# Gated linear attention and a two-layer MLP on one core: two tokens to a partition, one logarithm for both, quarter-tile scores, single PSUM banks, five early loads on ScalarE's DMA ring

## The chip, the cores and the metric

The kernel runs on one core of a Trainium2 chip. The metric is the device time of one execution in microseconds, and less is better. The profile is one execution taken by the hardware profiler; its span is measured from the first to the last instruction. The engines are named as in the profile: PE (TensorE), PEld (its weight loads), DVE (VectorE), ACT (ScalarE), POOL (GpSimd) and SP (SyncE).

## The reference

There are 4 batches, 8 heads, 768 tokens and 48 channels per head. Attention is a recurrence with a forget gate per channel; its output, with the heads side by side, goes through a layer of 384 to 2048, a smooth gate, and a layer of 2048 to 384.

```python
f = 1.0 / (1.0 + np.exp(-f_logit))
for t in range(S):
    state = f[:, :, t, :, None] * state + einsum('bhd,bhe->bhde', k[:, :, t], v[:, :, t])
    y[:, :, t] = einsum('bhd,bhde->bhe', q[:, :, t], state)
x = y.transpose(0, 2, 1, 3).reshape(B * S, H * D)
h = x @ w_in
g = 0.5 * (h + np.sqrt(h * h + 4.0))
return g @ w_out
```

## The kernel before

The 3072 tokens are cut into 24 blocks of 128 tokens, one token to a partition, and two blocks make a pair p (12 pairs, three to a batch). `add_load` reads f, q, k and v of a pair, each with two DMAs of 128 partitions x 8 heads x 48 floats, so each piece in memory is 192 bytes (L363).

**Logs and decays.** `add_logs` takes the exponential of -f (L425) and ln(1 + that) (L430), both over 768 columns, on ACT, and splits the result into a high (L433) and a low (L436) 16-bit part. `add_decays` sums the logarithms along the block with a centred triangular matrix on PE (L467, L468) into `hps`, adds small matmuls with `hvec` for the sums of each half block (L473, L474), takes exponentials of the sums with both signs on ACT (`ea` and `eap`, L481), and multiplies q by one and k by the other (`qk`, L487). v is cast to 16 bits (L494). `add_gammas` turns the half-block sums into the decay of the state from block to block (`nls` L499, `gi` L538, `gam` L547).

**Attention.** `add_attention` transposes q and k of a block, on PE (L593, copy L597) for pairs 0 to 4 and by DMA (L581) for pairs 5 to 11. Scores of two heads at a time go to two PSUM tiles (`sc`, L618: matmuls of 48 rows, in the upper and in the lower half of the array), are masked on DVE (`pm`, L625), and are multiplied by v; a term with the state is added (`y`, L639 and L641). `add_state` forms the next state (`u` L703 and L706, `sn` L710). y is cast (L648 or L650) and transposed, on PE (L683, L686) or by DMA (L673), into `xT`.

**MLP.** `add_mlp1` runs eight half steps per pair, each of six matmuls of 256 columns (L740). ACT squares the result (`hsq`, L746) and takes the square root of two half steps at a time (`r`, L755), and DVE joins them to the gated value (`g`, L763). `add_mlp2` multiplies by `w_out` in four quarters of four matmuls of 384 columns for each block (`o`, L780), copies the sum to `o_sb` on ACT or DVE (L789, L791), and stores it (L795).

**Order.** No scheduler of the language is at work. A planner of the kernel, `Plan`, is given each piece of work with its engine, a duration, what it depends on and a due time from the tables `BASE` and `SHIFT`; it plays the engines forward, and then the pieces are emitted in the order found. The engine of a piece that has a choice is in the table `ENG`. Loads, DMA transposes and stores share SP's queue, in order; weights are loaded and cast by POOL's queue (L388). PSUM is divided into pools, five banks for `hps`, two for attention, one for `o`:

```python
NH, NA, NO = 5, 2, 1
```

f has three load buffers, and q, k and v have four each; `o_sb` has two buffers of one block. ACT changes its function table between exponential/logarithm and square root where the planner's order asks for it (L841, L843).

Of the kernel before, what the change touches and what calls it, by code (L numbers as in the profile page):

```python
# [15 lines left out]
GROUPS = [[0], [1], [2], [3], [4], [5, 6], [7, 8], [9, 10], [11]]  # L16

XBAR = [5, 6, 7, 8, 9, 10, 11]

BASE = {  # L20
    "A": [-91.5, -48.2, -86.7, 59.5, 5.1, 3.6, 35.4, 93.4, 55.3, 161.2, 112.5, 128.2],
    "B": [-33.0, -23.9, 18.0, -28.5, -32.3, 71.1, -18.2, 43.6, 49.9, 25.6, 129.6, 106.7],
    "M": [63.0, -3.2, -1.9, 48.3, 21.6, 51.8, 114.9, 66.8, 229.7, 86.1, 210.4, 238.2],
    "O": [63.2, 45.4, 128.9, 46.1, 124.2, 143.7, 179.0, 123.5, 212.6, 237.4, 202.6, 191.4],
}
PART = {n: k for k, v in {
    "A": "W hi lo qk v16 nls gam", "B": "T SC KV Y Yc YT xq xy", "M": "M1 M R G", "O": "M2 ev out"}.items()
    for n in v.split()}

SHIFT = {  # L30
    "ld": 25.6, "win": 4.5, "wout": 7.0, "W": -4.7, "hi": 73.7, "lo": -32.1, "qk": -11.9, "v16": -32.1,
    "nls": -54.3, "gam": -112.9, "T": -87.4, "xq": -171.2, "SC": 9.3, "Y": -140.2, "Yc": 36.7, "YT": 70.6,
    "xy": 89.2, "KV": 58.5, "M1": 3.8, "M": 94.0, "R": -53.7, "G": -57.6, "M2": 33.2, "ev": -104.7,
    "out": 212.9,
}

NEAR = {'PE': 0.02, 'ACT': 0.1, 'DVE': 0.05, 'POOL': 0.3, 'SP': 0.2}

ENG = {
    "hi": "DDDDPDPPPPPP",  # L40
    "lo": "PPPDPPPDPPPD",
    "qk": "PPPPDPDDPDPP",
    "v16": "PDPPDPPPPPPP",
    "T": "DDADDDDDDDAAADDADDADDDDD",
    "Yc": "AADDADDDDDDDDDADDDDDDDDD",
    "ev": "DDDDDADDDDDDDADADAADAAAA",
}
FULL = {"D": "DVE", "A": "ACT", "P": "POOL"}

FINE = [0]  # L50

START = {"POOL": 3.8, "DVE": 3.6, "PE": 3.4, "ACT": 0.7, "SP": 0.7}

AFTER = {'in': 0, 'out': 2}


NH, NA, NO = 5, 2, 1

WDMA, VDMA = True, False

ORDER = "P0 P1 i03 f2 i47 o07 qkv2"


class Op:
    __slots__ = ("eng", "dur", "deps", "emit", "due", "allocs", "uses", "end", "kind", "dma", "ins", "flow", "issued")

    def __init__(self, eng, dur, emit, deps=(), due=0.0, allocs=(), uses=(), kind=None, dma=None, ins=()):
        self.eng, self.dur, self.emit, self.due, self.kind, self.dma = eng, dur, emit, due, kind, dma
        self.deps = [d for d in deps if d is not None]
        self.allocs, self.uses = list(allocs), list(uses)  # L70
        for b in self.uses:
            b.users.append(self)
        self.end = None
        self.ins = list(ins)
        self.flow = None


class Ring:
    def __init__(self, n, ordered):
        self.n, self.bufs, self.ordered, self.made = n, [], ordered, 0  # L80


class Buf:
    def __init__(self, ring):
        self.ring, self.users = ring, []
        self.seq = ring.made
        ring.made += 1


class Plan:  # L90

    HOP = 0.22
    TABLE = 1.3

    def __init__(self):
        self.queues = {}
        self.order = []

    def add(self, queue, eng, dur, emit, p=None, at=None, due=0.0, **kw):
        if isinstance(dur, dict):
            eng = FULL[ENG[queue][p if at is None else at]]
            dur = dur[eng]
        due += SHIFT.get(queue, 0.0) + (0.0 if p is None else BASE[PART[queue]][p])
        op = Op(eng, dur, emit, due=due, **kw)
        self.queues.setdefault((eng, queue), []).append(op)
        return op

    def ready(self, op):  # L110
        t = 0.0
        for d in op.deps:
            if d.end is None:
                return None
            t = max(t, d.end + (0.0 if d.eng == op.eng and d.dma is None else self.HOP))
        for b in op.allocs:
            r = b.ring
            k = len(r.bufs) - r.n
            if r.ordered and b.seq != len(r.bufs):
                return None  # L120

            k += sum(1 for x in op.allocs[:op.allocs.index(b)] if x.ring is r)
            if k >= 0:
                for u in r.bufs[k].users:
                    if u.end is None:
                        return None
                    t = max(t, u.end + (0.0 if u.eng == op.eng and u.dma is None else self.HOP))
        return t

    def flows(self):  # L130


        todo = {"SP": [], "POOL": []}
        for op in self.order:
            if not isinstance(op, str) and op.dma is not None:
                todo[op.eng].append([op.issued, op.dma[0], op])
        t = 0.0
        while todo["SP"] or todo["POOL"]:
            live = {e: q[0] for e, q in todo.items() if q and q[0][0] <= t + 1e-9}
            later = [q[0][0] for e, q in todo.items() if q and e not in live]  # L140
            if not live:
                t = min(later)
                continue
            rate = {"SP": 0.35, "POOL": 0.65} if len(live) == 2 else {e: 1.0 for e in live}
            step = min([x[1] / rate[e] for e, x in live.items()] + [a - t for a in later])
            t += step
            for e, x in live.items():
                x[1] -= step * rate[e]
                if x[1] <= 1e-9:
                    x[2].flow = t + x[2].dma[1] - x[2].issued  # L150
                    todo[e].pop(0)

    def run(self, passes=3):
        for n in range(passes):
            for ops in self.queues.values():
                for op in ops:
                    op.end = None
                    for b in op.uses + op.allocs:
                        b.ring.bufs = []
            self.order = []  # L160
            self.once()
            if n + 1 < passes:
                self.flows()

    def once(self):
        heads = {k: 0 for k in self.queues}
        free = dict(START)
        dma_free = 0.0
        table = None
        left = sum(len(v) for v in self.queues.values())  # L170
        by_eng = {}
        for k in self.queues:
            by_eng.setdefault(k[0], []).append(k)
        stretch = None
        loose = False
        while left:
            best = None
            for eng, ks in by_eng.items():
                now = free.get(eng, 0.0)
                cands = []  # L180
                for k in ks:
                    if heads[k] < len(self.queues[k]):
                        op = self.queues[k][heads[k]]
                        t = self.ready(op)
                        if t is not None:
                            cands.append((max(now, t), op, k))
                if not cands:
                    continue
                if eng == "PE" and stretch is not None and not loose:

                    if any(heads[k] < len(self.queues[k]) and self.queues[k][heads[k]].kind == ("W", stretch)
                           for k in ks):
                        cands = [c for c in cands if c[2][1] != "M1" or not c[1].allocs]
                        if not cands:
                            continue
                if eng == "ACT" and stretch is None and not loose:

                    opened = []
                    for c in cands:
                        if c[1].kind is not None and c[1].kind[0] == "W":  # L200
                            ins = [d for o in self.queues[c[2]][heads[c[2]]:heads[c[2]] + 16]
                                   if o.kind == c[1].kind for d in o.ins]
                            if any(d.end is None for d in ins):
                                continue
                            c = (max([c[0]] + [d.end - 1.0 for d in ins]),) + c[1:]
                        opened.append(c)
                    cands = opened
                    if not cands:
                        continue
                if eng == "ACT":  # L210

                    if stretch is not None and not loose:
                        mine = [c for c in cands if c[1].kind == ("W", stretch)]
# [662 lines left out]
```

## Time and profile before

The time before is 229.51 us, the median of two runs (228.28 to 230.74).

| | from the profile |
|---|---|
| span | 228.4 us, 4796 instructions |
| busiest engines | PE 186.2, ACT 168.7, DVE 157.0, POOL 75.1 us |
| mean granted PE clock | 0.963 |
| DMA | 129303 packets, 32.10 MB, 121088 of the packets under 512 B |
| ACT table loads | 16, of 1283 ns each |
| first matmul of the first layer | at 24.16 us |

A busy time is the union of an engine's instructions. A matmul's end is modelled, so a busy PE is not a PE at its peak. Where a row gives a mean for matmuls, it is longer than the distance from one start to the next, because they overlap. An idle engine costs something only where it is the one the others wait for.

### The profile page before, as it was taken

The page shows a single profiled execution, that of the slowest core. Times are in us where ns is not written, and L with a number is a line of the kernel's source. Part 1 is how long each engine was busy: PE and PEld are TensorE (multiplying, and loading weights), DVE is VectorE, ACT ScalarE, POOL GpSimd, SP SyncE. Part 2 cuts the span into 40 slices and gives each one's busy share as a digit, 9 for nine tenths or more (in the row PEclk, how much of TensorE's full clock was granted, in tenths as well). Part 3 has the DMA queues.
Part 4 walks back from the last instruction along what each step waited for, and adds up shares of the span by engine and source line. Part 5 has one row for each costly group of instructions (what it writes and reads, how often), then busy time and mean ns, then how long its engine had stood idle before and what let it go on. Part 6 is the DMA issues. An engine that isn't in the chain of part 4 may idle for free.

```text
span 228.4 us, 4796 instructions
## 1 busy us (share of the span) xinstructions
PE 186.2 (82%) x1870; PEld 133.3 (58%) x1870; DVE 157.0 (69%) x295; ACT 168.7 (74%) x258; POOL 75.1 (33%) x74
## 2 busy tenths in 40 slices
PE   0456858589998499599449999699999999999983
PEld 0243636357666257477326766576777777777641
DVE  6154286699895469598155998489989899855420
ACT  5333395999999918399705998599799999999820
POOL 5799426560640449610000692012504200000000
PEclk9999997999999589999967999999999999999999
DMA  7999999999998998999980569411193532010101
GB/s 140 207 194 188 178 208 181 204 155 202 189 222 170 230 209 175 247 171 220 220 207 1 124 139 207 102 52 55 52 195 76 119 47 57 17 54 34 70 34 69
DMA packets 129303, 32.10 MB, mean 141 GB/s; under 512 B 121088, under 2 KB 129280, under 8 KB 129280
## 3 DMA queue, kind: packets, MB, share of 16 engines
q1 hardware_dynamic: 123904, 28.65, 63.6%
q0 software_dynamic: 5376, 3.15, 9.5%
q8 instruction: 14, 0.23, 0.4%
q14 instruction: 9, 0.07, 0.1%
HBM read 25.17 MB, written 4.72 MB: 131 GB/s over the span
## 4 chain that ended last, share of the span: by engine, by line
PE 57%; ACT 16%; DVE 7%; DMA 6%; POOL 5%; SPq 4%; issue 3%; POOLq 0%; ACTq 0%; DVEq 0%
PE o L780 23%; PE hps L740 22%; ACT hsq L746 5%; DMA out_dram<-o_sb 4%; ACT r L755 4%; SPq L363 4%; PE sc L618 2%; DMA xT<-y 2%; DVE pm L625 2%; POOL w_in L388 2%; POOL qk L487 2%; PE hps L468 2%; ACT L843 2%; PE hps L467 1%; PE y L641 1%
## 5 line engine op out<-in xcount | busy, mean ns | idle before, releaser
L780 PE MATMUL o<-w_out,g 128*128 128x384 f16 x384 | 76.0, 335 | 14.7 <-DVE o_sb L791 13.5
L740 PE MATMUL hps<-xT,w_in 128*128 128x256 f16 x576 | 75.0, 282 | 3.7 <-DMA xT<-y 2.3
L763 DVE SCALAR_TENSOR_TENSOR g<-hps,r 128x512 f16<-128x512 f32 x96 | 61.6, 683 | 12.7 <-ACT r L755 12.3
L746 ACT ACTIVATE hsq<-hps 128x512 f16<-128x512 f32 x96 | 53.8, 591 | 22.0 <-PE hps L740 21.0
L740 PEld LDWEIGHTS <-w_in 128*128 128x128 f16 x576 | 56.7, 101 | 15.8 <-issue 5.0
L780 PEld LDWEIGHTS <-g 128*128 128x128 f16 x384 | 36.3, 100 | 34.8 <-issue 17.5
L755 ACT ACTIVATE r<-hsq 128x1024 f16<-128x1024 f16 x48 | 50.7, 1057 | 1.3
L625 DVE TENSOR_TENSOR pm<-sc,mask 128x512 f16<-128x512 f32 x48 | 31.1, 683 | 9.0 <-PE sc L618 9.0
L494 POOL CAST v<-ld_v 128x768 f16<-128x768 f32 (+1 forms) x11 | 8.5, 771 | 57.6 <-PE y L641 36.8
L487 POOL TENSOR_TENSOR qk<-ld_q,ea 128x768 f16<-128x768 f32 (+1 forms) x9 | 14.7, 1631 | 34.9 <-ACT ea L481 33.5
L481 ACT ACTIVATE ea<-hps 128x384 f32<-128x384 f32 x24 | 10.6, 491 | 12.1 <-PE hps L474 12.1
L791 DVE COPY o_sb<-o 128x384 f32<-128x384 f32 x15 | 8.3, 554 | 15.7 <-DMA out_dram<-o_sb 14.9
L436 POOL TENSOR_TENSOR llo<-ls,lhi 128x768 f16<-128x768 f32 (+1 forms) x10 | 15.3, 1534 | 9.8 <-DVE gam L547 6.2
L487 POOL TENSOR_TENSOR qk<-ld_k,eap 128x768 f16<-128x768 f32 (+1 forms) x9 | 15.4, 1712 | 0.0
L425 ACT ACTIVATE ld_f<-ld_f 128x768 f32<-128x768 f32 (+1 forms) x13 | 10.5, 804 | 4.6 <-DMA ld_f<-in_f_logit_dram 4.6
L467 PE MATMUL hps<-lhi,wcent 128*128 128x384 f16 x24 | 8.9, 370 | 5.8 <-DVE lhi L433 5.8
L618 PE MATMUL sc<-qkT 48*128 48x128 f16 x192 | 11.0, 228 | 2.4 <-DVE pm L625 1.1
L710 DVE TENSOR_TENSOR sn<-u,gam 128x384 f16<-128x384 f32 x20 | 11.0, 549 | 2.4 <-PE u L706 2.3
L641 PE MATMUL y<-v,pm 128*128 128x48 f16 x192 | 11.8, 187 | 0.4 <-DVE pm L625 0.4
L597 DVE COPY qkT<-tr 128x1024 f16<-128x1024 f16 x9 | 6.0, 685 | 8.7 <-PE tr L593 8.7
L641 PEld LDWEIGHTS <-pm 128*128 128x128 f16 x192 | 10.2, 99 | 3.0 <-issue 1.3
L618 PEld LDWEIGHTS <-qkT 48*128 48x128 f16 x192 | 6.2, 98 | 9.5 <-issue 8.0
(55 smaller groups left out, 217.5 us busy)
## 6 DMA issues: line engine op xcount, KB each, us to landing
ld_f<-in_f_logit_dram SPq DMA_DIRECT2D x24, 192.0 KB, 4.0
ld_q<-in_q_dram SPq DMA_DIRECT2D x24, 192.0 KB, 3.8
ld_k<-in_k_dram SPq DMA_DIRECT2D x24, 192.0 KB, 3.8
ld_v<-in_v_dram SPq DMA_DIRECT2D x24, 192.0 KB, 3.9
out_dram<-o_sb SPq DMA_DIRECT2D x24, 192.0 KB, 2.2
w_in<-in_moe_w_in_dram POOLq DMA_DIRECT2D x8, 192.0 KB, 7.7
w_out<-in_moe_w_out_dram POOLq DMA_DIRECT2D x8, 192.0 KB, 6.8
qkT<-qk SPq DMA_TRANSPOSE x14, 3.3
```

Source lines behind the costliest of these rows:

```text
L436: eng_of[lg[p, x].eng].tensor_tensor(out=llo[p % NL][:, x:y, :, 0:D], in0=T["ls", p][:, x:y], in1=lhi[p % NL][:, x:y, :, 0:D], op=ALU.subt ...
L467: nc.tensor.matmul(out=ca, lhsT=wcent, rhs=lhi[p % NL][:, r, :, 0:D], start=True, stop=False)
L487: eng_of[mu[p, x, i].eng].tensor_tensor(out=qk[p % NB][:, x:y, i, :, 0:D], in0=T[name, p][:, x:y], in1=T[e, p][:, x:y], op=ALU.mult)
L618: nc.tensor.matmul(out=T["sc", r, s][:, j, :], lhsT=qkT[o:o + D, NP + j, :], rhs=qkT[o:o + D, j, :], start=True, stop=True)
L625: nc.vector.tensor_tensor(out=T["pm", r][:, s], in0=T["sc", r, s], in1=mask16.unsqueeze(1).broadcast_to([128, NP, C]), op=ALU.mult)
L641: nc.tensor.matmul(out=y[:, j, s], lhsT=T["pm", r][:, s, j, :], rhs=T["v16", p][:, i, 2 * j + s, :], start=(c == 0), stop=(c == 0 or s == 1))
L710: nc.vector.tensor_tensor(out=T["sn", r + 1], in0=T["u", r], in1=gam[b % 2][:, c].unsqueeze(3).broadcast_to([128, NP, 2, D]), op=ALU.mult)
L740: nc.tensor.matmul(out=hb[:, a, :], lhsT=w_in16[j2][:, j, a * 128:(a + 1) * 128], rhs=T["xT", p][:, j, :], start=(j == 0), stop=(j == NJ - 1))
L746: nc.scalar.activation(out=T["hsq", p, j4][:, a], in_=T["h", p, j2], func=AF.Square, scale=1.0)
L755: nc.scalar.activation(out=T["r16", p, j4], in_=T["hsq", p, j4], func=AF.Sqrt, scale=0.25, bias=1.0)
L763: nc.vector.scalar_tensor_tensor(out=T["g", p][:, jn:jn + 2, :].rearrange("p a t -> p (a t)"), in0=T["h", p, 2 * j4 + a], scalar=0.5, in1= ...
L780: nc.tensor.matmul(out=T["o", p, i], lhsT=T["g", p][:, jn, i * C:(i + 1) * C], rhs=w_out16[jn // 2][:, jn % 2, :], start=(jn == 0), stop=( ...
```

## The change

Nothing in the result changes, but the work is cut in another way, and the planner is gone: the order of all pieces, the engine of each, and the PSUM banks of each that needs some are written out as a list of words (`ORDER`), which is played through once. `lq0.0:A` means the load of q, pair 0, first half, issued by ACT; `cu0.0:T@01` means the cumulative sums on PE into banks 0 and 1.

**Two tokens to a partition.** A pair of 256 tokens is loaded with one DMA for each of f, q, k and v. Partition p holds tokens 2p and 2p+1, which lie side by side in memory, so a piece is 384 bytes. Partitions 0 to 63 hold the first 128 tokens, and 64 to 127 the others. The loads have three buffers each.

**One logarithm for both.** With e = exp(-f), u = 1 + e is formed for both tokens (`ut`), multiplied together (`tt`), and one logarithm is taken of the product, so cumulative sums and their exponentials are of two-token steps. What the single tokens lack is multiplied in directly: q of the even token by the odd one's u (`qu`), k by u or by the product (`ku`), before the old multiplications by the exponentials (`qm`, `km`).

**Quarter-tile scores.** A score matmul has 48 rows and 64 columns of weights, for a head of two and for one of the two blocks, so four lie side by side in the array. Transposes, v products and state updates use the upper or lower 64 rows.

**Single banks.** Every PSUM tile is one of eight banks, named in the order. **Five early loads** (`lq0.0`, `lq0.1`, `lv0.0`, `lv0.1`, `lq1.0`) are issued by ACT ahead of its first exponential. DMA transposes serve pairs 4 to 11 instead of 5 to 11. A pair's output is stored from a buffer of both blocks, of which there are two, in two DMAs of 64 partitions.

```diff
-GROUPS = [[0], [1], [2], [3], [4], [5, 6], [7, 8], [9, 10], [11]]
-XBAR = [5, 6, 7, 8, 9, 10, 11]
-NH, NA, NO = 5, 2, 1
+XBAR = [4, 5, 6, 7, 8, 9, 10, 11]
+DEPTH = {'f': 3, 'q': 3, 'k': 3, 'v': 3, 'UT': 2, 's': 2, 'ep': 2, 'ea': 2, 'v16': 4, ... 'xT': 5, 'hsq': 2, 'r16': 2, 'g': 4, 'os': 2}
+ORDER = """
+lf0.0:S lf0.1:S lf1.0:S lk0.1:S lk0.0:S TABLE:e lq0.0:A lq0.1:A lv0.0:A lv0.1:A lq1.0:A ex0.0:A ut0.0:P ex0.1:A tt0.0:D
...
+"""
...
+                    eng(e).dma_start(out=T[s, p][:, hs].rearrange("p h i d -> p h (i d)"),
+                                     in_=src[s][bb][hs, t0:t0 + 256, :].rearrange("h (p i) d -> p h (i d)", i=2))
...
+                eng(e).tensor_scalar(out=T["UT", p][:, 0::2, hs], in0=T["f", p][:, hs].rearrange("p h i d -> p i h d"),
+                                     scalar1=1.0, scalar2=None, op0=ALU.add)
...
+                mul(e, u[:, 1, hs], u[:, 0, hs], u[:, 2, hs])
...
+                nc.scalar.activation(out=T["s", p][:, hs], in_=T["UT", p][:, 1, hs], func=AF.Ln)
...
+                t = T["q", p][:, hs, 0, :]
+                mul(e, t, t, T["UT", p][:, 2, hs])
...
+                t = T["k", p][:, hs].rearrange("p h i d -> p i h d")
+                mul(e, t, t, T["UT", p][:, 0:2, hs])
...
+                for j in range(4):
+                    for h in range(2):
+                        for cc in range(2):
+                            r = slice(64 * h, 64 * h + D)
+                            t = T["qkT", p, cc]
+                            nc.tensor.matmul(out=T["sc", p, i, h][64 * cc:64 * cc + 64, j, :],
+                                             lhsT=t[r, 1, j, i, :], rhs=t[r, 0, j], start=True, stop=True)
```

## The prediction

> **What bounds the kernel now.** I read the busy table first, then the 40 slices, then a table of stretches, the waits and the chain.
>
> ```profile
> PE 186.2 (82%) x1870; PEld 133.3 (58%) x1870; DVE 157.0 (69%) x295; ACT 168.7 (74%) x258; POOL 75.1 (33%) x74
> ...
> PE   0456858589998499599449999699999999999983
> ...
> PEclk9999997999999589999967999999999999999999
> DMA  7999999999998998999980569411193532010101
> ```
>
> TensorE (PE) is the longest engine, yet 42.2 us of the span are left on it. From the 22nd slice on (120 us) it has nines, but for one slice and the tail; before that it has holes, and there the DMA row is full.
>
> ```profile
> 0.00:24.00 24.00, 9.93 (x102) 6.52 (x103) 11.79 (x34) 9.28 (x18) 19.96 (x31) 1.00 1.06 182
> 24.00:60.00 36.00, 28.61 (x300) 20.52 (x300) 26.68 (x50) 30.16 (x45) 15.06 (x15) 0.95 1.12 188
> 60.00:97.00 37.00, 29.66 (x313) 21.21 (x312) 25.54 (x50) 27.27 (x44) 19.73 (x15) 0.91 1.01 208
> 97.00:120.00 23.00, 16.68 (x151) 11.94 (x150) 14.55 (x27) 15.21 (x21) 0.82 (x1) 0.92 1.16 204
> ...
> 148.00:180.00 32.00, 32.00 (x354) 23.07 (x353) 29.31 (x54) 29.31 (x46) 8.77 (x6) 1.00 0.40 83
> 180.00:218.00 38.00, 38.00 (x353) 28.79 (x352) 27.65 (x46) 33.63 (x48) 0.00 (x0) 1.00 0.22 55
> ```
>
> The columns are stretch, length, busy us of PE, PEld, DVE, ACT, POOL, clock, DMA share, GB/s. From 148 to 218 PE has no idle time. From 0 to 120 it lacks 14.1 + 7.4 + 7.3 + 6.3 = 35.1 us, with DMA above 1.0 throughout and about 200 GB/s. No compute engine is full there. What PE waits for:
>
> ```profile
> DVE o_sb L791 <- DMA out_dram<-o_sb: 14.9, 3, 7.1
> PE o L780 <- DVE o_sb L791: 13.5, 4, 6.2
> PE hps L467 <- DVE lhi L433: 5.8, 1, 5.8
> PE tr L593 <- POOL qk L487: 4.7, 4, 2.0
> ```
>
> The chain joins the first two: from 65.9 to 73.5 us SyncE issues loads (L363), then a store of 3.24 us lands, then the copy to o_sb runs (76.82), then PE goes on (77.43). A store sits in the same in-order queue behind loads that are held up by the full DMA, and `o` has one PSUM bank and `o_sb` two buffers. The same happens at 92.9 and 113.3.
>
> **How much PE work there is.** In the dense stretch six first-layer matmuls (L740) take 0.65 us and four second-layer ones (L780) 0.65 us, in the chain. 96 groups of each make 96 x 0.655 x 2 = 125.8 us. From 148 to 218 there are 268 matmuls of L740 and 180 of L780 (29.3 + 29.5 = 58.8 us), which leaves 11.2 us for about 3.5 pairs of attention, 3.2 us a pair. TensorE transposes of five pairs add about 1.2 each. Dense work: 125.8 + 12 x 3.2 + 6 = 170 us. The span is this, the head, the tail, and holes.
>
> **What the Trainium skill says.** (1) "DMA: Bandwidth & Descriptors", Specifications, gives 512 B as the smallest transfer at line rate. The loads here are 192 B pieces (48 floats) and 121088 of 129303 packets are under 512 B; about 200 GB/s at a full DMA share agrees. (2) "TensorEngine Tiling (Array Packing)", Key Properties, says that tiles run independently but that a change of tiling mode drains the array. The chain agrees: L740 x6 after scores (L618) takes 0.76 us, otherwise 0.65, so 0.11 us a change and back. (3) "GPSIMD Engine Reference", Engine selection, calls two-input operations about twice as slow there as on VectorE: L487 is 1812 to 1917 ns on POOL, 981 to 1101 on DVE. (4) "Trainium Kernel Development and Optimization", Key Constraints: a further issuing queue saves issue time only, as the DMA engines are shared. The trace of before has one hardware ring only, so it doesn't show this.
>
> **Loads.** Two neighbouring tokens of one head now lie in a partition, so a piece is 384 B and the load packets fall from 98,304 to 49,152. Loads are 18.9 MB; at 190 GB/s, unchanged, they take 99 us, and at an unchanged packet rate half, 50 us. I take 75. Stores and weights stay; the DMA transposes are 24 instead of 28, for 8 pairs instead of 7, about the same data. DMA remains busy, but no longer saturated up to 120 us. Stores get two buffers of a whole pair instead of two of a half pair, and `o` may take any of eight banks, so a late store no longer stops PE: of 14.6 us (PE after o_sb, both engines) I keep 2. Bound: 0 to 14.6.
>
> **ScalarE.** One logarithm for two tokens: 12 of 384 instead of 768 columns, 10.3 to about 6.5 us. Exponentials of the cumulative sums (L481): 48 of 384 become 24, 21.3 to 10.9. Table loads 16 to 10, at 1.28: -7.7. More copies of y and o go to it: 26 instead of 13 at 0.475, +6.2. Transposed copies, hi, xT and a half v: +3.4. Sum -3.8 - 10.4 - 7.7 + 6.2 + 3.4 = -12, from 168.7 to **157**. The Square and Sqrt passes (53.8 and 50.7) don't change. Most of it is off PE's path.
>
> **VectorE and GpSimd.** The logarithm of a product needs 1+e (ut), a product (tt), and q and k multiplied by these (qu, ku) before the old products (qm, km). In units of a two-input pass of 384 columns: before 50 on POOL (45.4 us, 0.91 each); by the order of the changed kernel 65.5, at 0.95 this is 62. One-input passes: 19 of 768 at 0.83 and a few halves, 19. Weight issues 12.4, the small decays, stores and constants 8. POOL becomes **102 us** (from 75). On DVE the same kind adds 41.5 x 0.5 = 21 and 8 more of small passes; gone are lo, hi, v and qk (17), nls and gi/gam (13), and half the y, o, qkT and xT copies (11): **145 us** (from 157). Masks and gates (31.1 and 61.6) stay. Neither is the longest engine; POOL's load matters because the last pair's keys (km) must come some 67 us before the end: after them PE still has about 4.7 pairs of first and 5.5 of second layer, 53 us, 3 attentions, 10, and the tail.
>
> **TensorE.** The program has 2321 matmuls for 1870, as keys, values and scores are cut into half and quarter tiles. If the parts overlap fully this costs nothing; if each costs an issue slot (hvec pairs start 26 ns apart) it is 451 x 26 ns = 12 us. The parts of a score have the same 128 columns and four may run together, so I take 4. More mode changes: 12 kv, 12 yt, 5 transposes at 0.11, +3. Gone: 96 small hvec matmuls at 0.026, -2.5, and one pair of transposes, -1.2. Dense work 170 + 3.5 = about **174** (170 to 183).
>
> **Head and tail.** First-layer work starts at 24.16 us now. ScalarE issues five loads ahead of its first exponential; SyncE's early issues are 0.53 to 0.9 us, so it starts at about 5.5 instead of 3.70. This wait costs, since ut, tt, ln, hi, lo queue behind it; but q and v of pair 0, which wait their turn on SyncE now (the first v cast on POOL starts at 10.41 us, released by its load), come earlier. Adding up durations down the order for pair 0 (exponential 0.52, ut 0.5, tt 0.3, ln 0.35, hi 0.35, lo 0.5 and hops 0.2, second half to 9.2; sums and four exponentials 11.6; qm on POOL 13.2; transposes and copies 14.4; four masks behind other DVE work 18; y, its copy and transposes 20.5) gives first-layer work at about **20.8** (19 to 24), with 6 us of PE's work behind it. The last copy and store take 0.48 + about 3 us, 3.6 as now.
>
> **Sum.** 20.8 + (174 - 6) + 3.6 = 192.4 if dense. Remaining holes: 2 for o, 3 for a lower clock (the clock of 0.91 to 0.95 from 24 to 120 costs 7 now), 6 for waits like those on POOL and ACT (15 now). **203 us.**
>
> **Rivals.** (a) The forecast, chance 0.55: 203. (b) Dense: parts overlap fully and no holes but the clock, 20.8 + 164 + 3.6 + 3 = 191; for it speaks 148 to 218, against it that this stretch had no loads and little POOL work. Chance 0.15. (c) GpSimd sets the pace: 102 us, 15% slower by sharing with VectorE and with 30 us of waits (it now waits 33.5 for ea alone), 4 + 117 + 30 = 151, and 67 after it: 218. For it: every pair needs ku, qu and qm in turn on one engine. Chance 0.2. (d) Slower: the holes are not the loads' but those of a fixed order; all of 42 us of idle time stays, PE gains 12 by issue slots and 3 by drains, and five issues on ScalarE add 2 to the head: 228.4 + 17 = 245. For it: banks named one by one and three load buffers instead of four for q, k, v tie PE to the slowest reader. Chance 0.1. Against it is the o wait, which has a plain cause that goes away.
>
> **Numbers.** 203; range 190 to 224, from (b) to just above (c), leaving (d) and a little of (b) out. Faster 0.87, same 0.04, slower 0.09: (c) gives 0.03 to same, (d) 0.01.
>
> **Right or wrong.** DMA share should drop under 1 before 100 us; SyncE's loads should not hold stores, so waits of o on copies should be under 3 us; ACT about 157, DVE 145, POOL 102 us; first-layer matmuls from 20.8; PE with nines from about 30 us. A PE busy over 195, or POOL in nines with km as what PE or SyncE waits for, would show (d) or (c).

## The result and the profile after

The changed kernel takes **219.9 us** (219.5 to 220.3) against 229.5: a ratio of 0.9655, with a 95% interval of 0.9573 to 0.9738. It is faster, as forecast, but by 3.5% and not by 11.5%. Its profiled span is 218.5 us. The kept trace of the version with all products on VectorE (experiment 3) is of an execution 2.2% slower than the fastest of that version. First the busy table and three rows of the slices (each 5.5 us) of the changed kernel:

```profile
PE 179.6 (82%) x2320; PEld 128.3 (59%) x2320; DVE 161.5 (74%) x284; ACT 154.9 (71%) x252; POOL 118.5 (54%) x128
...
PE   0217884878688999994998589999889999999991
...
POOL 3599489199993995597999930789000000000002
...
DMA  7999999259991679999998999981991017102204
```

ACT is where it was forecast (154.9 for 157). DVE is 161.5 instead of 145 and POOL 118.5 instead of 102. The DMA row has gaps in the 8th and the 13th slice, which it had not before, but PE has nines only from the 14th slice on (71 us), not from 30 us, and a four and a five at 98 and 120 us. POOL's row has nines from 44 to 66 us and from 104 to 126. The span fell by 9.9 us: PE's busy time by 6.6 and its idle time by 3.3 (from 42.2 to 38.9). The table of stretches, with the same columns as before the change:

```profile
0.00:24.00 24.00, 8.20 (x144) 6.00 (x144) 17.55 (x47) 8.39 (x19) 18.23 (x31) 1.00 1.15 239
24.00:60.00 36.00, 27.29 (x365) 18.69 (x363) 26.95 (x49) 29.43 (x45) 27.49 (x29) 0.95 0.96 170
60.00:97.00 37.00, 35.50 (x535) 25.51 (x533) 32.94 (x56) 30.17 (x51) 28.29 (x27) 1.00 0.87 185
97.00:120.00 23.00, 19.42 (x270) 13.78 (x268) 17.87 (x28) 17.10 (x27) 21.61 (x20) 1.00 1.01 181
120.00:148.00 28.00, 24.72 (x331) 17.48 (x332) 25.14 (x40) 21.26 (x38) 16.57 (x18) 0.94 0.97 182
148.00:180.00 32.00, 30.59 (x438) 22.64 (x436) 22.97 (x39) 22.54 (x36) 4.60 (x5) 1.00 0.44 71
```

From 24 to 120 us PE lacked 21.0 us before; now it lacks 8.7 + 1.5 + 3.6 = 13.8. The first stretch is worse (15.8 instead of 14.1), and the last two rows, of 60 us, now lack 4.7 instead of 2.3. Traffic fell from 188 and 208 to 170 and 185 GB/s between 24 and 97 us, and rose from 117 to 182 between 120 and 148 us. The waits:

```profile
DVE UT L136 <- POOL UT L182: 9.6, 5, 3.6
PE ps L221 <- POOL hl L133: 9.2, 1, 9.2
...
PEld L440 <- DMA win<-in_moe_w_in_dram: 4.6, 3, 3.3
...
PE ps L440 <- DMA win<-in_moe_w_in_dram: 3.8, 2, 3.0
...
PE ps L440 <- DVE pm L341: 3.1, 2, 1.9
```

TensorE's waits for copies of `o`, 14.6 us before, are gone but for 1.4 us, in which other work waits for a bank that `os` reads. In their place PE and its weight loads wait for first-layer weights (3.8 and 4.6), and PE for a bank that a mask still reads (3.1); VectorE waits for `ut` on GpSimd (9.6). The single wait of 9.2 us is the start: the first cumulative sums (L221) begin that late, where they waited 5.8 us before. Two rows of the groups show what such passes cost (after the bar: busy us, mean ns of one):

```profile
L182 POOL TENSOR_SCALAR UT<-f 128x768 f32<-128x768 f32 (+1 forms) x10 | 21.3, 2132 | 10.7 <-ACT f L175 7.3
...
L136 DVE TENSOR_TENSOR UT<-UT 128x384 f32<-128x384 f32 (+1 forms) x10 | 7.7, 782 | 9.8 <-POOL UT L182 9.6
```

One `ut` takes 2132 ns on GpSimd, and a product of 384 columns on VectorE 782 ns, two halves counted in. The forecast had 830 and 500. Of the chain that ended last, the part around the first layer (start, length, what):

```profile
18.55 2.31 DVE q L136
...
24.34 3.14 issue
27.48 0.42 POOL UT L182
27.90 1.67 issue
29.57 5.92 DMA win<-in_moe_w_in_dram
...
35.54 1.46 PE ps L440 x6
```

The engine that issues the weights is GpSimd. Its queue is in order; at 24.34 us it stands still for 3.14 us in front of pair 3's `ut`. The trace names no releaser for this wait ("issue"); by the timelines the `ut` needs an exponential that ScalarE runs only at 26.48, behind copies of pair 0's y, and starts as that ends. Then comes the `ut` itself, and only at 29.57 the next weight issue, which lands 5.92 us later, and PE goes on at 35.54.

### The profile page after: what moved, and what is told of

It reads as the page before. It is cut to its first block, busy times and chain, and to the rows that moved or that the text cites. A ratio compares the mean times of both kernels' runs of the same rounds, so it can differ in the third digit from the quotient of the medians.

```text
span 218.5 us, 5662 instructions
## 1 busy us (share of the span) xinstructions
PE 179.6 (82%) x2320; PEld 128.3 (59%) x2320; DVE 161.5 (74%) x284; ACT 154.9 (71%) x252; POOL 118.5 (54%) x128
## 3 DMA queue, kind: packets, MB, share of 16 engines
q10 hardware_dynamic: 3152, 1.18, 2.5%
## 4 chain that ended last, share of the span: by engine, by line
PE 42%; DVE 15%; POOL 11%; DMA 11%; ACT 10%; issue 6%; SPq 2%; POOLq 0%; ACTq 0%; DVEq 0%
PE ps L440 17%; PE ps L477 17%; POOL UT L182 6%; DMA wout<-in_moe_w_out_dram 4%; ACT r L455 3%; ACT hsq L449 3%; DMA win<-in_moe_w_in_dram 3%; DVE qk L136 3%; DVE UT L136 3%; DVE q L136 3%; DMA qkT<-qk 2%; DMA f<-in_f_logit_dram 2%; PE ps L334 2%; DVE pm L341 2%; POOL wout L145 2%
## 5 line engine op out<-in xcount | busy, mean ns | idle before, releaser
L440 PE MATMUL ps<-xT,win 128*128 128x256 f16 x576 | 73.5, 277 | 6.9 <-DMA win<-in_moe_w_in_dram 3.8
L465 DVE SCALAR_TENSOR_TENSOR g<-ps,r 128x512 f16<-128x512 f32 x96 | 62.2, 683 | 21.2 <-ACT r L455 21.0
L477 PE MATMUL ps<-wout,g 128*128 128x384 f16 x384 | 71.2, 327 | 3.0 <-DMA wout<-in_moe_w_out_dram 3.0
L440 PEld LDWEIGHTS <-win 128*128 128x128 f16 x576 | 55.5, 99 | 18.7 <-DMA win<-in_moe_w_in_dram 4.6
L449 ACT ACTIVATE hsq<-ps 128x512 f16<-128x512 f32 x96 | 53.7, 594 | 14.9 <-PE ps L440 14.1
L341 DVE TENSOR_TENSOR pm<-ps,mask 128x512 f16<-128x512 f32 x48 | 30.8, 680 | 5.0 <-PE ps L334 4.9
L182 POOL TENSOR_SCALAR UT<-f 128x768 f32<-128x768 f32 (+1 forms) x10 | 21.3, 2132 | 10.7 <-ACT f L175 7.3
L221 PE MATMUL ps<-hl,tri 128*128 128x384 f16 (+1 forms) x52 | 12.6, 360 | 12.3 <-POOL hl L133 9.2
L136 POOL TENSOR_TENSOR k<-k,UT 128x768 f32<-128x768 f32 (+1 forms) x12 | 21.1, 1764 | 2.6 <-DVE g L465 2.6
L136 POOL TENSOR_TENSOR qk<-q,ea 128x384 f16<-128x384 f32 (+1 forms) x16 | 16.1, 1027 | 0.2
L221 PEld LDWEIGHTS <-tri 128*128 128x128 f16 x52 | 5.3, 108 | 16.3 <-issue 8.2
L334 PE MATMUL ps<-qkT 48*64 48x128 f16 x384 | 10.2, 228 | 3.5 <-DVE qkT L133 1.0
L334 PEld LDWEIGHTS <-qkT 48*64 48x64 f16 x384 | 6.6, 110 | 7.6 <-issue 4.8
```

The source lines that it names most:

```text
L136: eng(e).tensor_tensor(out=o, in0=a, in1=b, op=ALU.mult)
L182: eng(e).tensor_scalar(out=T["UT", p][:, 0::2, hs], in0=T["f", p][:, hs].rearrange("p h i d -> p i h d"), scalar1=1.0, scalar2=None, op0=A ...
L221: nc.tensor.matmul(out=o, lhsT=K["tri"][:, m], rhs=hl[:, r, hs, 0:D], start=(r == 0), stop=(r == 1))
L334: nc.tensor.matmul(out=T["sc", p, i, h][64 * cc:64 * cc + 64, j, :], lhsT=t[r, 1, j, i, :], rhs=t[r, 0, j], start=True, stop=True)
L341: nc.vector.tensor_tensor(out=T["pm", p, i, h], in0=T["sc", p, i, h], in1=K["mask"][:, i].unsqueeze(1).broadcast_to([128, 4, 128]), op=ALU ...
L440: nc.tensor.matmul(out=T["h", p, m][:, a], lhsT=K["win"][m][:, j, a * 128:(a + 1) * 128], rhs=T["xT", p][:, :, j, :], start=(j == 0), stop ...
```

## The experiments

All ratios are against the kernel before, run on the same chip. In the diffs of the order, `:P`, `:D`, `:A`, `:S` name GpSimd, VectorE, ScalarE and SyncE, `ut` is 1 + e, `wi` a first-layer weight load, `qm` and `km` the products with the exponentials.

**1. `ut` off GpSimd; weights ahead of `ut`; both.** Three runs on one chip. The first moves every `ut` to VectorE:

```diff
-ut0.0:P ... ut2.0:P ... ut3.0:P ... ut4.0:P ... ut5.0:P ...
+ut0.0:D ... ut2.0:D ... ut3.0:D ... ut4.0:D ... ut5.0:D ...
```

> All forming of 1+e (ut) goes from GpSimd to VectorE, where the changed kernel's own trace has 618 ns for 768 columns against 2238 on GpSimd. Nothing else moves. If GpSimd's slow ut is what the forecast missed, GpSimd falls from 118.5 to about 98 us busy, VectorE rises from 161.5 by 9 x 0.6 + 0.4, about 6, the waits of VectorE and SyncE on ut go, and the time falls by 5 to 12 us, to 208 to 215. If the late weights or the order hold the kernel, the time stays within 2 us of 219.9.

The second moves three weight issues only:

```diff
-ut3.0:P ... wi5:P ... wi6:P ... wi7:P
+wi5:P wi6:P wi7:P ut3.0:P
```

> In GpSimd's queue the last three issues of first-layer weights (wi5, wi6, wi7) go ahead of ut of pair 3, into the 3.14 us in which GpSimd waits for the exponential of that pair. If weights stuck behind that wait are what holds the first layer, the PE waits on win (3.8 us, and 4.6 on its weight loads) go and the time falls by 3 to 6 us, to 214 to 217. If the first layer is only brought forward into a later wait (for second-layer weights, or for GpSimd), the time stays within 1.5 us of 219.9.

The third makes both edits.

> Both: ut on VectorE and the three weight issues ahead of the wait. If the two causes are separate, the gains add, to 205 to 212 us. If both are the one queue of GpSimd, ut on VectorE alone lets the weights out in time, and this is as fast as ut on VectorE alone, within 1.5 us.

Measured: `ut` on VectorE 214.6 us, ratio 0.9391 (0.9336 to 0.9446), apart from the changed kernel's interval. The weights alone: 218.7 us, 0.957 (0.9514 to 0.9626), not apart from it, although their last issue went from 33.2 to 25.9 us. Both: **212.4 us**, 0.9277 (0.922 to 0.9334), just below `ut` alone, so the weight issues count once `ut` is off GpSimd. A row of the tile UT in the first of them (min/median/max ns, first and last start us, forms):

```profile
L182 DVE TENSOR_SCALAR UT<-f x13: 352/550/1317, 6.6 to 112.6; 128x768 f32<-128x768 f32 x11, 128x384 f32<-128x384 f32 x2
```

The same pass, with a median of 2135 ns on GpSimd in the changed kernel, takes 550 on VectorE. POOL falls from 118.5 to 98.2 us, while DVE stays at 162.0 (about 6 more were expected). With both edits, GpSimd's timeline shows the weights out before the next wait:

```profile
22.21 3.09 POOL L142 DMA_DIRECT2D win<-in_moe_w_in_dram  x4
30.12 0.50 POOL L133 CAST hl<-s 128x384 f16<-128x384 f32 x1 [4.82 <-ACT s L196]
```

The wait of 4.82 us is still there, but no weight stands behind it: the waits for `win` fall from 3.8 (PE) and 4.6 (weight loads) to 0.9 and 1.2 us. By the stretches, PE's idle time from 24 to 180 us falls from 18.5 to 11.8 us and its work before 24 us grows by 0.9, together 7.6 of the 7.7 us by which the span fell (218.5 to 210.8). So 7.5 of the 16.9 us between forecast and result (8.7 if the ratios are compared) came from `ut` and the issues in one queue.

**2. What an addition costs on GpSimd, and what the two engines cost each other.** A kernel that computes nothing of the reference: rows of six instructions of one kind, on one engine alone and then on both at once.

```python
for _ in range(6):
    mul(g)
    mul(d)
meet()
for _ in range(6):
    plus(g, UV, f)
    mul(d)
```

> This kernel computes nothing of the reference: it runs single operations in rows of six, one engine at a time and then two at once, and writes constants out. Three questions. (1) Why ut takes 2.2 us on GpSimd: if the permuted writing is the cause, the same addition into contiguous columns, or as two three-dimensional halves, takes about 0.9 us, as the cast of 768 columns does, and a permuted copy is as slow as ut; if the addition of a constant is the cause, all three forms of it take about 2.2 us and the permuted copy 0.9. (2) Whether VectorE's products of two tensors and GpSimd's work exclude each other: if so, a product of 384 columns takes 0.55 us alone and 1.0 to 1.5 beside products or casts on GpSimd, and the two engines take the sum of their times; if the long ones in the trace had another cause (waits not shown), it stays at 0.55 to 0.6. (3) Whether a weight issue on GpSimd holds a product on VectorE: 0.55 if not, over 1 if so.

GpSimd's timeline (start, us of the row of six): a constant added to 768 floats; a copy of them, in two layouts; a product of 384, alone and beside VectorE's:

```profile
31.58 13.18 POOL L52 TENSOR_SCALAR UV<-f 128x768 f32<-128x768 f32 x6
44.82 5.24 POOL L68 COPY UV<-f 128x768 f32<-128x768 f32 x6
50.01 5.24 POOL L70 COPY UT<-f 128x768 f32<-128x768 f32 x6
...
60.43 6.34 POOL L56 TENSOR_TENSOR po<-pa,pb 128x384 f32<-128x384 f32 x6
...
75.55 7.32 POOL L56 TENSOR_TENSOR po<-pa,pb 128x384 f32<-128x384 f32 x6
```

VectorE's: six products alone, beside GpSimd's products, beside its additions, beside its casts; then twelve beside weight issues:

```profile
67.55 3.52 DVE L56 TENSOR_TENSOR do<-da,db 128x384 f32<-128x384 f32 x6
...
74.99 7.03 DVE L56 TENSOR_TENSOR do<-da,db 128x384 f32<-128x384 f32 x6
...
83.22 4.68 DVE L56 TENSOR_TENSOR do<-da,db 128x384 f32<-128x384 f32 x6
...
97.11 6.66 DVE L56 TENSOR_TENSOR do<-da,db 128x384 f32<-128x384 f32 x6
...
112.25 7.07 DVE L56 TENSOR_TENSOR do<-da,db 128x384 f32<-128x384 f32 x12
```

An addition takes 13.18 / 6 = 2.2 us and a copy 0.87; the layout makes no difference. So the cast's price was the wrong row for `ut`. And a product of 0.59 us on VectorE takes 1.17 beside GpSimd's products (1.11 beside casts, 0.78 beside additions), while GpSimd's go from 1.06 to 1.22. The two weight issues that fell into the row of twelve (0.98 and 0.78 us) cost VectorE nothing (0.59).

**3. All `qm` and `km` on VectorE**, from the version with both edits of 1 and the two small ones of 4.

```diff
-qm0.1:P ... qm3.0:P ... km3.0:P ... qm4.0:P ... km5.0:P ... qm5.0:P ...
+qm0.1:D ... qm3.0:D ... km3.0:D ... qm4.0:D ... km5.0:D ... qm5.0:D ...
```

> The kernel with all four edits, and all products qm and km that GpSimd forms (27 passes of 384 columns) given to VectorE. In the runs with ut on VectorE its 41.5 passes of two inputs take 0.81 to 0.88 us each, 0.55 where GpSimd is idle. If VectorE is held by GpSimd's operations on the shared memory path, the price of a pass falls to about 0.65 as GpSimd has 28 us less to do, VectorE's busy time rises by only 8 to 13 us (to 170 to 175) and the time stays within 2 us. If the price is VectorE's own, its busy time rises by over 20 us (over 182) and the time rises by 3 us or more.

The ten products u x u, which are on VectorE in both, in the version it was made from:

```profile
L136 DVE TENSOR_TENSOR UT<-UT 128x384 f32<-128x384 f32 (+1 forms) x10 | 8.3, 845 | 0.1
```

And in this one:

```profile
L136 DVE TENSOR_TENSOR UT<-UT 128x384 f32<-128x384 f32 (+1 forms) x10 | 5.8, 597 | 0.1
```

The mean falls from 845 to 597 ns, with nothing changed in these instructions but what GpSimd does meanwhile: its busy time fell from 97.4 to 67.8 us. Masks, which read PSUM, take 680 ns in both traces, so VectorE as such was not faster. It has 27 more products, 16 us at 0.59, and is only 8.8 us longer busy. This agrees with sharing in the kernel itself, though not every row follows: the seven `lo` passes on VectorE (L207) went from 800 to 888 ns. The ratio is 0.9341 (0.9251 to 0.9431) against 0.9242 (0.9191 to 0.9293) for the version it was made from: no gain. The intervals overlap, so a loss isn't shown either.

**4. The early loads, the tail, and the order around pair 0.** The five early loads on SyncE instead of ScalarE, from the changed kernel:

```diff
-lk0.0:S TABLE:e lq0.0:A lq0.1:A lv0.0:A lv0.1:A lq1.0:A ex0.0:A
+lk0.0:S lq0.0:S lq0.1:S lv0.0:S lv0.1:S lq1.0:S TABLE:e ex0.0:A
```

> The five early loads are issued by SyncE, after the first two of k, instead of ScalarE. If the second ring helps (issue time of five loads saved on SyncE), the first pair's q and v land later and the time rises by 1 to 3 us. If the load of q1 in front of the first exponential (which started at 6.09 us here, 3.70 before) was what made the head late, the exponential starts before 5 us and the time falls by 1 to 2 us.

The first exponential starts at 3.46 instead of 6.09 us and the first layer at 25.07 instead of 26.87, but the ratio is 0.9706 (0.9653 to 0.976): not to be told from the changed kernel. Then, on the version with both edits of 1, the last stores on SyncE (`st11.0.0:P` to `:S`, and two more), pair 1's `qu` behind pair 0's masks, and the two together:

> The same kernel (212.4 us), but the three last stores that GpSimd issues are issued by SyncE. From the last PE instruction to the end the changed kernel takes 6.5 us, where the forecast took 3.6; the last issues on GpSimd take 0.55 us each and SyncE's 0.34. If GpSimd's issue and its queue's slower start cause the longer end, the time falls by 1 to 2 us; if it is the four half stores themselves, it stays within 0.5 us.

> The same kernel (212.4 us), but on VectorE the product qu of pair 1 comes after the masks of pair 0, just before its use. In the changed kernel it took 2.31 us on the chain in front of the masks, since GpSimd was at work. If the sharing of VectorE and GpSimd makes the head late, the first layer starts 1.5 to 2.5 us earlier and the time falls by 1 to 2 us; if the weights then hold the first layer, its start moves but the time stays within 0.7 us.

> The kernel with ut on VectorE and earlier weights, the last stores on SyncE, and the late qu of pair 1, all four. The two last edits gave 1.0 and 1.6 us by themselves, each inside its uncertainty. If they are real and separate, this runs at 209 to 210.5 us; if they were chance, at 211.5 to 212.5.

Ratios 0.9225 (0.9144 to 0.9305), 0.9238 (0.9178 to 0.9298) and 0.9242 (0.9191 to 0.9293) beside 0.9277: none is told apart, and the first layer starts at 25.4 to 25.7 us in the last two, as before (25.57). So `qu` in front of the masks was not what holds the start, nor GpSimd's stores the end: it takes 4.3 us after the last matmul with them on SyncE and 4.5 without. (The 6.5 us in the expectation count from the last matmul on the chain; from the last matmul of all it is 4.6 in the changed kernel.) On the last of them: f and q of pair 1 behind pair 0's loads; with that, pair 1's exponential, `ut`, `tt`, logarithm and its split behind pair 0's products, transposes and scores; and this second step with the loads as they were:

```diff
-lf0.0:S lf0.1:S lf1.0:S lk0.1:S lk0.0:S TABLE:e lq0.0:A ... lv0.1:A lq1.0:A ex0.0:A
+lf0.0:S lf0.1:S lk0.1:S lk0.0:S lf1.0:S lq1.0:S TABLE:e lq0.0:A ... lv0.1:A ex0.0:A
```

```diff
-ln0.1:A lo0.0:D ex1.0:A hi0.1:P ... lo0.1:P ut1.0:D ku0.1:P cu0.1:T@01 tt1.0:D ea0.1:A
+ln0.1:A lo0.0:D hi0.1:P ... lo0.1:P ku0.1:P cu0.1:T@01 ea0.1:A ... ex1.0:A ... ut1.0:D tt1.0:D
```

> The kernel with all four edits; besides, of the ten loads that start together, the two of pair 1 come last: f1 after k of pair 0, and q1 on SyncE instead of ScalarE. In the kernel with four edits the first exponential starts at 6.32 us and the first layer at 25.72. If the crowd of loads is what makes the first f late (it landed 2.9 us after its issue in the kernel before, 4.4 in the changed one), the exponential starts at about 5 us, the first layer at 24.5 and the time falls by about 1 us, within its uncertainty. If it is the sharing of queues by two rings whatever their order, the exponential stays at 6 us.

> As the kernel with f first (210.5 us, first exponential at 4.69, first layer at 25.57), and in the written order pair 1's exponential, ut, tt, logarithm, hi and sums come behind pair 0's products, transposes and scores. If the order held pair 0 behind pair 1's load, the transposes of pair 0 start at about 12 us instead of 15, the first layer at 22 to 23.5, and the time falls by 1 to 3 us. If pair 0's own chain is the limit, the first layer stays at 25 to 26 us and the time within 1 us.

> The same order of pair 0 before pair 1, but the ten early loads as in the changed kernel (f of pair 1 third, q of pair 1 on ScalarE). If both the crowd of loads and the order count, the first layer starts about 1.5 us later than in the run with f first, at 23.5 to 25. If the order alone counts, both start alike.

Ratios 0.9212 (0.9118 to 0.9305), 0.9139 (0.9074 to 0.9205) and 0.9193 (0.9121 to 0.9264); the first layer starts at 25.57, 24.62 and 26.03 us, each about 1 us later than expected. PE's timeline of the second, with both steps:

```profile
12.45 0.29 PE L310 MATMUL ps<-ident,qk 64*128 64x64 f16 x4 [2.82 <-DVE qk L136]
...
15.66 1.06 PE L334 MATMUL ps<-qkT 48*64 48x128 f16 x31 [0.61 <-DVE qkT L133]
16.66 0.50 PE L221 MATMUL ps<-hl,tri 128*128 128x384 f16 x1
18.14 1.12 PE L221 MATMUL ps<-hl,tri 128*128 128x384 f16 x3 [0.98 <-DVE hl L207]
...
20.12 0.82 PE L353 MATMUL ps<-v,qk 64*128 64x96 f16 x16 [0.68 <-ACT v L131]
...
24.62 2.61 PE L440 MATMUL ps<-xT,win 128*128 128x256 f16 x16
```

The transposes (L310) now start at 12.45 us, where they start at 14.99 in the version it was made from two steps before, but of these 2.5 us only 1.1 reach the first layer (25.72 to 24.62), and by the timeline cumulative sums of pair 1 (L221) still wait for VectorE between pair 0's scores (L334) and its products with v (L353). And the span does not follow (208.1 for 207.6): PE does 1.1 us more before 24 us and idles 12.8 instead of 9.8 us from there to 180. What is brought forward goes into later waits.

**5. The waits of the kernel before, alone.** In the kernel before, six buffers for `o_sb` instead of two, with the same order:

```diff
-                T["o_sb", p, i] = sp.tile([128, DM], FP32, name="o_sb", tag="o_sb", bufs=2)
+                T["o_sb", p, i] = sp.tile([128, DM], FP32, name="o_sb", tag="o_sb", bufs=6)
```

> The kernel before with six o_sb buffers instead of two, in the same order on every engine. The wait of VectorE on stores (14.9 us) goes, and with it most of PE's 14.6 us on o. If late stores held PE, as the forecast took for 12.6 us of its gain, the time falls by 8 to 13 us from 229. If the loads that held the stores hold the work after them as well, PE only waits later, and the time falls by less than 4 us.

219.5 us, 0.9624 (0.9561 to 0.9687). The stretches from 60 to 120 us in which the waits were:

```profile
60.00:97.00 37.00, 32.81 (x368) 23.91 (x367) 31.94 (x60) 33.11 (x53) 20.63 (x16) 1.00 1.01 208
97.00:120.00 23.00, 18.44 (x208) 13.29 (x205) 19.42 (x35) 19.40 (x30) 6.45 (x5) 0.99 1.06 205
```

PE does 32.8 and 18.4 us there where it did 29.7 and 16.7, with the DMA share still over 1.0 and 192-byte pieces. The wait was a real one, four more buffers take it away, and this one edit brings as much as the whole change does (0.9655), within the intervals.

**6. The size of the pieces, alone.** On the version with both edits of 1, each load of f, q, k and v as two DMAs of 192-byte pieces; nothing else differs.

```diff
-eng(e).dma_start(out=T[s, p][:, hs].rearrange("p h i d -> p h (i d)"),
-                 in_=src[s][bb][hs, t0:t0 + 256, :].rearrange("h (p i) d -> p h (i d)", i=2))
+for i in range(2):
+    eng(e).dma_start(out=T[s, p][:, hs, i],
+                     in_=src[s][bb][hs, t0:t0 + 256, :].rearrange("h (p i) d -> i p h d", i=2)[i])
```

> The kernel with ut on VectorE and earlier weights (212.4 us), but each load is two DMAs, one for each of the two tokens of a partition, so pieces are 192 B again and packets number as before. If the piece size is what relieves the DMA, its share returns above 1.0 up to about 120 us and the time rises by 6 to 15 us; this includes 47 more issues of about 0.4 us on SyncE. If the DMA wasn't the limit, the time rises by less than 3 us.

The rows of the version it was made from (slices of 5.3 us), then its own (5.5 us):

```profile
PE   0317887779899699999989599999989999999991
...
DMA  6999999399990999999989999936960029011314
```

```profile
PE   0033888879998979769979899669989999999991
...
DMA  7999999999999899989989999990992016202204
...
DMA packets 132058, 32.88 MB, mean 149 GB/s; under 512 B 123936, under 2 KB 131984, under 8 KB 132032
```

224.5 us, 0.9841 (0.9781 to 0.9902), for 0.9277: 5.6% of the kernel before, 12 to 13 us, lie in the pieces and in the second issue of each load together. The run does not divide them: SyncE's issues have 13% of this run's chain, 2% in the version it was made from. With 50,000 packets more for the same bytes the DMA row has no gap before the 28th slice, and PE has its holes up to there.

## Why the prediction was half right

**The bound, the waits on `o`, the pieces.** These held in the main. Waits on copies of `o` are gone but for 1.4 us, and in the kernel before they were worth 8 us (experiment 5; the forecast had 12.6). The pieces, with the issues, are worth some 12 us (6). The DMA share fell under 1.0 from 24 to 97 us, as foreseen, though not in the head (1.15) or from 97 to 120 (1.01). But that sign does not show what it was meant to show. One of SyncE's waits is this (L168 issues the loads):

```profile
SPq L168 <- DVE qk L136: 18.8, 3, 16.1
```

In the longest, SyncE issues no load from 30.5 to 46.7 us: by the order and the timelines the next one, q of pair 5, waits until a product of pair 2 has read its buffer, one of three. The gap in the 8th slice lies there, and the loads come later instead: from 120 to 148 us the share is 0.97, where it was 0.56. With both edits of 1, and the same larger pieces, the share is 1.03, 0.97 and 1.08 in the three stretches from 24 to 120 us.

**ScalarE and TensorE.** ACT came out at 154.9 for 157. In the dense part of the trace the 32 score matmuls of a pair take 0.57 us on the chain (0.64 once), where the 16 of before took 0.66: the parts overlap, and the 4 us for them were not needed.

**The sum.** Its terms against the trace: the head is 26.9 us instead of 20.8. From the first first-layer matmul to the last matmul PE is busy for 169.0 us, where the forecast had 168 and 3 for a lower clock. It is idle for 18.1 us there, where the forecast had 8, that is 2 for `o` and "6 for waits like those on POOL and ACT". The end is 4.6 instead of 3.6. So, beside the head, the term of the sum that failed is these 6 us: they measure 16.7, the 18.1 without the 1.4 for `o`. In the kernel before the same reckoning gives 24.3 idle less 14.6 for `o`, 9.7 us (the forecast's "15 now" is reached only if the first wait of the head, 5.8, is added, which lies in the head's term). The change was to lower these waits, and it raised them.

**The step behind it that failed is "VectorE and GpSimd", in two prices.** First, `ut` was among the "One-input passes: 19 of 768 at 0.83", the price of a cast. It is an addition, and it takes 2.13 us here and 2.2 by itself (2). Ten of them take 21.3 us instead of about 8, which is 13.3 of the 16.5 us by which POOL was missed. Second, "41.5 x 0.5 = 21" on VectorE took its 0.5 from rows in which GpSimd had little to do. The number of passes was right; their durations add up to 38.2 us, 0.92 each, 17 more than forecast, and DVE missed by 16.5. Alone a product takes 0.59 (2), so some 4 of the 17 us are the price itself and the rest is put down to sharing. The Trainium skill has the reason, in "SBUF — State Buffer", section "Who interferes with whom": a VectorE instruction with two inputs in SBUF contends with a GpSimd instruction that reads SBUF, since its second input comes through a read interface that the two share. Experiments 2 and 3 agree on the conflict. The page also calls the shared ports an exclusive lock, and with that experiment 2 does not agree: six and six products together take 7.9 us (74.99 to 82.87), and one row after the other would be 3.52 + 6.34 = 9.9.

**What it cost was not the busy time but the places in the queues.** Neither engine is the longest even now. The forecast had "Weight issues 12.4" as work on GpSimd, but not that each issue stands in order behind a 2.1 us pass and behind that pass's wait. Removing both took 7.5 us off (1): PE's idle time after the first first-layer matmul fell from 18.1 to 11.8 us, and the first layer started 1.3 us earlier. Rival (c), GpSimd sets the pace, said 218, and that this number fits is luck. Of its signs one was there: POOL in nines from 44 to 66 us and from 104 to 126. But it named `km` as what would be waited for, and those waits are for `ut` and the weights; and with GpSimd 20 us shorter (1) the time fell by 5 only.

**The head: 26.87 instead of 20.8.** The forecast had the last product of pair 0 at 13.2 us and first-layer work 7.6 later. In PE's timeline of the changed kernel:

```profile
15.70 0.77 PE L310 MATMUL ps<-ident,qk 64*128 64x64 f16 x16 [4.44 <-DVE qk L136]
...
18.60 0.64 PE L334 MATMUL ps<-qkT 48*64 48x128 f16 x15 [0.61 <-DVE qkT L133]
19.17 1.46 PE L221 MATMUL ps<-hl,tri 128*128 128x384 f16 x4
...
20.76 0.64 PE L334 MATMUL ps<-qkT 48*64 48x128 f16 x16
...
26.87 1.40 PE L440 MATMUL ps<-xT,win 128*128 128x256 f16 x6
```

The transposes start at 15.7, 2.5 us late: ScalarE starts its first exponential at 6.09 instead of 5.5, and half a `ut` on GpSimd takes 1.18 us instead of 0.5. From there it takes 11.2 us. By the chain the last copy of the transposes ends at 18.55 instead of 14.4 and the last mask at 23.27 instead of 18. So the lateness grows by 1.7 us over transposes and copies, by 1.1 over the masks and by 0.8 up to the first layer. Pair 1's cumulative sums (L221) lie between pair 0's two groups of scores, a product of pair 1 takes 2.31 us in front of pair 0's masks on VectorE (in the chain above), and pair 1's transposes take PE's last 1.0 us in front of the first layer. That this interleaving costs the time is read from the timelines and not shown: experiments on it moved the start by up to 1.1 us and the total by nothing that can be measured.

**What stays open.** With both edits of experiment 1 the span is 210.8 us, and the best versions have medians of 210.5 to 212.4: some 8 us above the forecast, 4 to 5 of them in the head. Whether a whole order made for the measured durations would reach 203 was not tried; single shifts did not. Nor was a fourth buffer for the loads, though SyncE still waits 10.6 us for one in the version with both edits and the DMA share is about 1.0 up to 120 us: that late loads hold the rest is neither shown nor excluded. The versions with both edits of 1, but for those of experiments 3 and 6, have ratios of 0.914 to 0.928 and beat both kernels, the one before by 7 to 9%, the changed one by 4 to 5%. Among them, only the interval of the version with the whole order of 4 (up to 0.9205) lies below that of experiment 1 (from 0.922), and not below those between.

## What to carry to other kernels

Price an operation by a row of its own kind on its own engine (an addition is not a cast on GpSimd), and price VectorE's two-input passes by rows in which GpSimd is as busy as it will be. Before moving work to an engine that has time left, look at what else is issued from its in-order queue and what stands behind the new work's wait: a weight load may cost more in its place than in its time. And where a wait has one plain cause, try the smallest edit for it first: here four more buffers brought as much as the rewrite did.

## What the runs showed of the hardware

On GpSimd an addition of a constant to 768 floats takes 2.1 to 2.2 us, 2.5 times a copy or a cast of them (0.87), in whatever layout. Products on VectorE and GpSimd at the same time slow VectorE by 2.0 (0.59 to 1.17 us) and GpSimd by 1.15 (1.06 to 1.22); beside GpSimd's additions VectorE is slowed by 1.3 only, and two weight issues from GpSimd left VectorE's products as they were (0.59). In the 2nd to 5th slice the version with both edits of 1 moves 247 to 261 GB/s with 384-byte pieces, and 178 to 217 with the same data in 192-byte pieces.
